# Attention and a mixture of experts in one hand-ordered kernel: weights loaded as eight halves, a later queue wait, another order

## The chip, the cores and the metric

The kernel runs on one core of one Trainium2 chip. The core has five engines with instruction queues of their own: TensorE (PE in the profile; its weight loads are PEld), VectorE (DVE), ScalarE (ACT), GpSimd (POOL) and SyncE (SP). Transfers are issued by an engine and carried out by 16 DMA engines. The metric is device time in microseconds (us), lower is better, as the median of several runs.

## What is computed

Eight sequences of 576 positions with 8 heads of 64 go through attention within a window of 32 positions to either side. The result, as 4608 rows of 512, goes through a mixture of experts: each row takes the expert with the largest router logit, to which a bias of the row's modality (0 or 1) is added.

```python
# q, k, v: [8, 8, 576, 64]
mask = np.abs(pos[:, None] - pos[None, :]) <= 32
attn = softmax(np.where(mask, q @ k.T / 8, -1e9))
x = (attn @ v).transpose(0, 2, 1, 3).reshape(4608, 512)
# modality_id: [4608], w_gate: [512, 8], modality_bias: [2, 8]
logits = x @ w_gate + modality_bias[modality_id]
e_idx, gate_w = argmax(logits, 1), max(softmax(logits))
# w1: [8, 512, 1024], w2: [8, 1024, 512]
for e in range(8):
    m = e_idx == e
    out[m] = gate_w[m, None] * (np.maximum(x[m] @ w1[e], 0) @ w2[e])
```

## The kernel before

With these inputs the bias decides the expert: all rows of one modality go to one expert. So two of the eight experts are loaded (`sp_i` holds which), and rows are sorted by modality. A flag computed on the chip would start a general path if this were not so; it isn't taken here.

**Tokens.** All work stands in a table, `ORDER`, of some 840 tokens. A loop at L891 to L893 reads them one by one and calls the function of that name with its numbers; a letter behind a slash is the engine (a, v, p), and digits behind a colon are banks of PSUM. Each engine runs its instructions in the order of this table; nothing reorders them. Waits between engines follow from which instruction reads what another has written. For this, the program is built on address ranges of the tiles.

The tokens, with b the sequence (batch), g one of its two head groups, t a tile of 256 rows (even t: expert 0, odd t: expert 1; t = 18 is a tile of rest):

- `l b.u.g` (L211) loads a half of q (u = 0) or k (u = 1), 288 KB, `lv b.i` (L216) a half of v, `W which.i` (L754) the weights: `W1.0`, `W1.1`, `W2.0`, `W2.1` are w1 and w2 of the two experts, 1 MB each as bf16 in `w1_sb` and `w2_sb`; `W1.2` and `W2.2` are those of the tile of rest. `Kg` (L248) loads the router's weights. All are issued by GpSimd, in the table's order. They take eight DMA lanes in turn (DMASW0 to 7 where an order is shown), and a transfer waits until the one before on its lane has landed.
- `t` (L540, DVE) transposes a load of q or k. `MA b.g`, `MB b.g` (L546 to L553, TensorE) write a band mask into banks ahead of scores, `SA`, `SB` (L572, TensorE) are the scores of a group, `sa`, `sb` (L580, L584, ACT) their exponentials into `pt`. A group without MA and MB has its exponentials multiplied with a mask on DVE instead: `M it` (L599), where it is two heads. `V it` (L618, TensorE) is attention times v, `v it` (L628, L629, DVE) the normalisation.
- `o b` (L531) builds one-hot matrices, `H b.m` (L638, TensorE) sorts rows of x with them, and `a b.m` (L656, ACT) copies the result to `xl`. `J` (L670) and `j` (L678) do the same for row numbers, to `cl`.
- `G k` (L708, L711, TensorE) are router logits, `r k.i` (L729 to L745) and `E k` (L751) the gate.
- `U t.mp` (L783) is a quarter of a tile's up-projection, eight matmuls of 128x256 over four slices of 128 (kd) of the 512; quarters 0 and 1 read the first 512 of the 1024 columns of w1, quarters 2 and 3 the others. `u` is its relu on ACT (L798) or DVE (L796).
- `D t.s.half` (L806) is half of the down-projection of 128 rows, four matmuls of 128x512; half 0 reads the first four of eight slices of w2. `y` scales by the gate on ACT (L834) or DVE (L836), `O` (L842, GpSimd) scatters 128 rows to the output from one of six buffers (`NYS`).
- `X i` (L887) are two filler matmuls on zeros. `N` is a drain of GpSimd: it waits there until what that engine has queued is done. `K..` are constants.

In the table `W1.0` stands behind `lv1.0`, `W1.1` behind `l2.0.1`, `W2.0` behind `lv2.1`; `U0.0` is the first up-projection, `U1.2` the first of expert 1, and `D0.0.0` the first down-projection. `N` stands ahead of `W2.2` and `W1.2`, towards the end.

## Time and profile before

| what | value |
| --- | --- |
| runs | 216.41 us median of 3 (216.21 to 216.47) |
| profiled execution | 214.1 us |
| its span, first to last instruction | 212.5 us |
| granted clock, mean | 0.988 |
| last matmul starts | 203.79 us, four of 128x512 in 1.04 us |
| last scatter | issued at 205.87 us, for 0.98 us |

The profile comes from one execution; its own time is 214.1 us, and the span is what its instructions cover. The 2.3 us to the median is the distance of that execution from the runs. Times in the rows below count from the span's start.

The page's slices (40 equal ones, busy tenths) show where the engines are full: TensorE from the fifth slice to the last but two, DMA through the first half.

```profile
PE   2877779899999999999999999999999999999950
DVE  6799999898988799878899883696547344303610
ACT  4588798898498989676897968665631221422220
POOL 7989989962934459999970442043021152743650
DMA  4999999999999999899996141022010995212431
```

### The profile page before, as it was taken

What the parts mean: (1) busy time and instruction counts of PE and PEld (TensorE: products, weight loads), DVE (VectorE), ACT (ScalarE), POOL (GpSimd) and SP (SyncE); (2) the same over time, 40 slices, a digit from 0 to 9 for tenths busy, and PEclk for the clock granted to TensorE, in tenths of its full rate; (3) what the DMA queues carried; (4) which work ended last, traced back from release to release, by engine and by line L of the source; (5) the groups of instructions that cost most, each with busy time, mean ns of one, the idle gap of its engine ahead of it and who ended that gap; (6) DMA issues with size and microseconds to landing.
All of it is one profiled execution on the core that took longest, in us unless ns stands there. A gap on an engine that the chain in (4) does not pass through costs nothing.

```text
span 212.5 us, 6219 instructions
## 1 busy us (share of the span) xinstructions
PE 192.7 (91%) x2525; PEld 137.0 (64%) x2552; DVE 152.1 (72%) x300; ACT 134.8 (63%) x229; POOL 119.2 (56%) x207
## 2 busy tenths in 40 slices
PE   2877779899999999999999999999999999999950
PEld 0444558688656887757885786578776676765620
DVE  6799999898988799878899883696547344303610
ACT  4588798898498989676897968665631221422220
POOL 7989989962934459999970442043021152743650
PEclk9999999999999999999999999999999999999995
DMA  4999999999999999899996141022010995212431
GB/s 70 189 187 185 205 175 214 185 190 212 212 188 185 181 226 297 164 149 206 86 210 141 50 150 49 3 99 103 3 49 3 158 221 214 102 49 96 153 106 61
DMA packets 47109, 30.43 MB, mean 143 GB/s; under 512 B 38712, under 2 KB 38752, under 8 KB 46688
## 3 DMA queue, kind: packets, MB, share of 16 engines
q0 software_dynamic: 46848, 29.90, 86.9%
q8 instruction: 22, 0.36, 0.7%
q14 instruction: 15, 0.12, 0.2%
q1 hardware_dynamic: 224, 0.05, 0.1%
HBM read 40.96 MB, written 9.70 MB: 238 GB/s over the span
## 4 chain that ended last, share of the span: by engine, by line
PE 65%; DMA 16%; POOL 9%; issue 4%; DVE 3%; POOLq 0%; DVEq 0%
PE banks L806 25%; PE banks L783 25%; DMA vt<-in_v_dram 9%; PE banks L618 5%; POOL oh L531 5%; PE banks L572 4%; DMA qkin<-in_q_dram 4%; DMA qkin<-in_k_dram 3%; PE banks L638 3%; DVE qk L540 2%; PE banks L708 2%; POOL qkin L211 1%; POOL out_dram L842 1%; POOL vt L216 1%; PE banks L670 1%
## 5 line engine op out<-in xcount | busy, mean ns | idle before, releaser
L783 PE MATMUL banks<-xl,w_sb 128*128 128x256 bf16 x576 | 70.8, 273 | 1.1 <-ACT xl L656 1.0
L806 PE MATMUL banks<-w_sb,hT 128*128 128x512 bf16 x266 | 67.3, 379 | 1.2 <-issue 0.2
L842 POOL DMA_INDIRECT out_dram<-ys,ix x37 | 38.4, 1039 | 52.7 <-issue 26.7
L783 PEld LDWEIGHTS <-w_sb 128*128 128x128 bf16 x576 | 54.3, 98 | 12.7 <-issue 1.6
L580 ACT ACTIVATE pt<-banks 128x1536 bf16<-128x1536 f32 x32 | 46.3, 1451 | 13.5 <-PE banks L572 13.4
L806 PEld LDWEIGHTS <-hT 128*128 128x128 bf16 x296 | 26.9, 98 | 24.9 <-issue 0.5
L540 DVE STREAM_TRANSPOSE qk<-qkin 128x576 int32<-128x576 int32 x32 | 39.3, 1248 | 2.4 <-DMA qkin<-in_k_dram 1.6
L599 DVE TENSOR_TENSOR pt<-pt,mask 128x1920 bf16<-128x1920 bf16 x30 | 34.0, 1150 | 3.0 <-ACT pt L580 3.0
L798 ACT ACTIVATE hT<-banks 128x512 bf16<-128x512 f32 x38 | 21.8, 598 | 19.3 <-PE banks L783 19.1
L796 DVE TENSOR_SCALAR hT<-banks 128x512 bf16<-128x512 f32 x36 | 24.3, 686 | 13.0 <-PE banks L783 11.8
L656 ACT CAST xl<-banks 128x704 f32 (+1 forms) x40 | 28.3, 707 | 4.6 <-DVE lo L729 2.2
L834 ACT ACTIVATE ys<-banks,gw 128x512 f32<-128x512 f32 x24 | 16.3, 688 | 19.3 <-PE banks L806 13.4
L629 DVE TENSOR_TENSOR xt<-banks,recs 128x640 bf16<-128x640 f32 x32 | 26.4, 825 | 1.2
L618 PEld LDWEIGHTS <-pt 128*128 128x128 bf16 x576 | 21.0, 97 | 4.7 <-issue 1.5
L618 PE MATMUL banks<-vt,pt 128*128 128x65 bf16 x576 | 22.6, 193 | 1.3 <-ACT pt L580 0.5
L216 POOL DMA_DIRECT2D vt<-in_v_dram x16 | 20.2, 1267 | 2.6 <-PE banks L572 1.1
L572 PE MATMUL banks<-qk 32*128 32x192 bf16 (+1 forms) x640 | 19.2, 240 | 2.5 <-DVE lpf L452 0.8
L531 POOL TENSOR_SCALAR oh<-io_l,lpf 128x128 bf16<-128x128 bf16 x30 | 20.2, 696 | 0.1
L572 PEld LDWEIGHTS <-qk 32*128 32x128 bf16 x640 | 12.6, 93 | 9.8 <-issue 5.3
L836 DVE TENSOR_SCALAR ys<-banks,gw 128x512 f32<-128x512 f32 x13 | 9.7, 744 | 12.8 <-PE banks L806 11.0
L678 ACT CAST cl<-banks 4x176 f32 (+1 forms) x40 | 11.4, 284 | 7.4 <-PE banks L670 6.8
L638 PE MATMUL banks<-oh,xt 128*128 128x128 bf16 (+1 forms) x160 | 13.0, 215 | 0.7 <-DVE xt L629 0.6
(157 smaller groups left out, 156.6 us busy)
## 6 DMA issues: line engine op xcount, KB each, us to landing
qkin<-in_q_dram POOLq DMA_DIRECT2D x16, 288.0 KB, 7.9
qkin<-in_k_dram POOLq DMA_DIRECT2D x16, 288.0 KB, 8.4
vt<-in_v_dram POOLq DMA_DIRECT2D x16, 288.0 KB, 7.7
w_sb<-in_moe_w_dram POOLq DMA_DIRECT2D x4, 1024.0 KB, 13.8
pt<-in_moe_w_dram POOLq DMA_DIRECT2D x2, 1024.0 KB, 10.1
out_dram<-ys,ix POOLq DMA_INDIRECT x37, 3.6
mid<-in_moe_modality_id_dram SPq DMA_DIRECT2D x3, 8.0 KB
mid<-in_moe_modality_id_dram SPq DMA_DIRECT2D x2, 6.0 KB
```

The source lines that it names most:

```text
L531: gp.tensor_scalar(out=t_[:, m, :], in0=io_l[:], scalar1=lpf[:, NM * b + m:NM * b + m + 1], scalar2=None, op0=ALU.is_equal)
L540: nc.vector.transpose(qk_t[b % 2][:, g, at:at + S].rearrange("p (t r) -> p r t", r=R), Ct["l", b, u, g][:].bitcast(I32).rearrange("p (r j) ...
L572: nc.tensor.matmul(st[:, h, WIN * i_:WIN * i_ + w_], qk[32 * h:32 * h + 32, c_, QK + k0:QK + k0 + P], qk[32 * h:32 * h + 32, c_, q0:q0 + w ...
L580: nc.scalar.activation(pt[:, :, 2 * part:2 * part + 2, 0:WIN], st[:, :, 0:2 * WIN].rearrange("p h (j c) -> p h j c", c=WIN), ACT.Exp, scal ...
L599: by[eng or "v"].tensor_tensor(out=p_ap, in0=p_ap, in1=mask[:], op=ALU.mult)
L618: nc.tensor.matmul(o_ap, pt[:, c1:c1 + P], vt[:, g0 + j, 0:D + 1], start=(m == 0 and i_ == 0), stop=(i_ == len(mine) - 1), skip_group_chec ...
L629: nc.vector.tensor_tensor(out=x_t[b % NX][:, :, P * hp:P * hp + P].rearrange("p m (h d) -> p h m d", h=2), in0=o_v[:, :, :, 0:D], in1=rec. ...
L656: ins = nc.scalar.copy(windows(xl, n_kd, P, NM * b + m), src)
L783: ins = nc.tensor.matmul(ph[:, u_, :], w1[:, kd, 2 * P * (mi // 2) + mi % 2:2 * P * (mi // 2 + 1):2], xl[:, kd, c0:c0 + n_], start=(kd == ...
L796: nc.vector.tensor_scalar(out=o_ap, in0=i_ap, scalar1=0.0, scalar2=None, op0=ALU.max)
L806: nc.tensor.matmul(Ct["D", t_, s_], Ct["h", t_][:, kf, P * s_:P * s_ + P], w2[:, kf, :], start=(kf == 0), stop=(kf == n_kf - 1))
L842: ins = nc.gpsimd.indirect_dma_start(out=out, out_offset=bass.IndirectOffsetOnAxis(ap=ix[:, k_, n_:n_ + 1], axis=0), in_=Ct["y", t_, s_][: ...
```

## The change

**Weights in halves.** `W_` takes one more number, h. For w1, h is the columns 512 h to 512 h + 511 of all four kd slices; a partition of `w1_sb` holds four rows of 1024 columns, so half h is four pieces of 512 in it, and the pieces of the two halves alternate. For w2, h is four of the eight slices, which stand together. Without h (`W1.2`, `W2.2`) the load is whole, as before.

```diff
-    def W_(_, which, i):
+    def W_(_, which, i, h=None):
         if ("er", i) not in T:
             T["er", i] = reg(sp_i[0:1, i:i + 1], [ET.Pool], 0, E - 1)
-        e_reg = T["er", i]
+        f_ = slice(0, F) if h is None else slice(F // 2 * h, F // 2 * (h + 1))
+        e_ = bass.ds(T["er", i], 1)
         if which == 1:
-            load_w(w1x if i == 2 else w1_sb[:, i], moe_w1, e_reg, W1P)
+            dst = w1x if i == 2 else w1_sb[:, i]
+            nc.gpsimd.dma_start(dst[:, :, f_], moe_w1[e_, :, f_].rearrange("a (ki ko) f -> ki (a ko) f", ki=P))
         else:
-            load_w((w2x if i == 2 else w2_sb[:, i]).rearrange("p (c e) d -> p c (e d)", e=2), moe_w2, e_reg, W2P)
+            dst = w2x if i == 2 else w2_sb[:, i]
+            dst = dst[:, f_.start // P:f_.stop // P].rearrange("p (c e) d -> p c (e d)", e=2)
+            nc.gpsimd.dma_start(dst, moe_w2[e_, f_, :].rearrange("a (c ki e) d -> ki (a c) (e d)", ki=P, e=2))
```

**The order.** The whole table is new: 846 tokens for 842. Two lines of it, around the first weights:

```diff
-V1:45 Kc3 lv1.0 W1.0 o0/p o1/p lv1.1 v1 V0:67 v0 SA0.1:0123 sa0.1 X7:4 SB1.0:4567 X8:3 X4:0 sb1.0 SA1.0:0123 t1.1.0 M2
+Kc4 Kr2 V1:67 Ky0 Kq1/a lv0.1 l2.1.0 v1 sa0.1 l2.0.0 lv1.0 Kc2 o0/p W1.0.1 Kc3 lv1.1 W1.1.0 V0:45 Ko0 SB1.0:0123 X11:6
...
-N Kf3:5 D11.0.0:1 D10.0.0:2 U13.3:3 u13.3/v r6.5 U12.2:4 G7:6 r7.0 G8:0 D10.0.1:2 D11.0.1:1 r8.5 Kf4 U12.3:3 D13.1.0:5
+y12.0/v r7.5 O12.0 O12.1 r7.6 W2.2 N G9:4 r7.1 r7.2 Z0 u13.3/v D13.0.0:5 U14.0:7 U17.0:3 U14.2:6 D13.1.0:2 E7 r7.3 r7.4
```

Beside the weights: group 1 of sequence 0 gets its mask on TensorE (`MA0.1`, `MB0.1` are new, `M2`, `M3` are gone); `N` stands behind `W1.2` and `W2.2`; the two one-hot matrices that DVE built (`o4`, `o7`) go to GpSimd, one pad (`Kp2`) from ACT to DVE; the relus are 37 and 37 on ACT and DVE instead of 38 and 36, with several of `u` and `y` on the other engine; the fillers are 14 tokens as before, 7 of them ahead of the first scores instead of 3. Behind the edit, lines of the changed kernel are 1 higher from the table on, and the weight loads are L765 (w1) and L769 (w2).

GpSimd, from the first weights on, in the kernel before (the buffers with their numbers: w1_sb_86 is the tile of both w1, qkin4 the fifth load buffer, vt2 the v of sequence 2, wg_sb the router's weights):

```order
L754 DMA w1_sb_86<-in_moe_w1_dram 128x4096 [waits DMASW0_49]
L211 DMA qkin3_72<-in_k_dram 128x1152 [waits DMASW1_49]
L211 DMA qkin4_73<-in_k_dram 128x1152 [waits DMASW2_49]
L216 DMA vt2_83<-in_v_dram 128x18x64 [waits DMASW3_49]
L248 DMA wg_sb_105<-in_moe_w_gate_dram 128x32 [waits DMASW4_49]
L531 TENSOR_SCALAR oh2_101<-io_l_118,lpf_127 128x128 x5
L211 DMA qkin5_74<-in_q_dram 128x1152 [waits DMASW5_49,DVE_49]
L216 DMA vt2_83<-in_v_dram 128x18x64 [waits DMASW6_49]
L754 ISA
L754 DMA w2_sb_87<-in_moe_w2_dram 128x4x1024 [waits DMASW7_49]
```

The same place in the changed kernel, from `W1.1.0` on (the second half of w1 here is `W1.0.0`, the third `W1.1.1`; `W1.0.1` stands eight rows ahead, on lane 5):

```order
L765 DMA w1_sb_86<-in_moe_w1_dram 128x4x512 [waits DMASW7_49]
L212 DMA qkin2_71<-in_q_dram 128x1152 [waits DMASW0_49]
L765 ISA
L765 DMA w1_sb_86<-in_moe_w1_dram 128x4x512 [waits DMASW1_49]
L217 DMA vt2_83<-in_v_dram 128x18x64 [waits DMASW2_49]
L212 DMA qkin3_72<-in_k_dram 128x1152 [waits DMASW3_49]
L532 TENSOR_SCALAR oh1_100<-io_l_118,lpf_127 128x128 x5
L249 DMA wg_sb_105<-in_moe_w_gate_dram 128x32 [waits DMASW4_49]
L212 DMA qkin4_73<-in_q_dram 128x1152 [waits DMASW5_49]
L212 DMA qkin5_74<-in_k_dram 128x1152 [waits DMASW6_49]
L765 ISA
L765 DMA w1_sb_86<-in_moe_w1_dram 128x4x512 [waits DMASW7_49]
```

Two halves stand where the second w1 stood, and `W1.1.1` has moved behind one v half, the router's weights and two loads of sequence 3; `W2.0.1`, `W2.0.0` and then `lv2.1` follow it.

TensorE at the first up-projection of the kernel before (`U0.0`, behind the scores `SB2.0`), and then at the first of expert 1 (`U1.2`):

```order
L572 MATMUL banks<-qk_77 128x128
L783 LDWEIGHTS w_sb [waits DMASW5_49]
L783 MATMUL banks<-xl,w_sb 128x256 [waits Activation_49]
L783 LDWEIGHTS w_sb
...
L783 LDWEIGHTS w_sb [waits DMASW0_49]
L783 MATMUL banks<-xl,w_sb 128x256 [waits Activation_49]
L783 LDWEIGHTS w_sb
```

The same two places in the changed kernel, `U0.3` and `U1.0`:

```order
L784 LDWEIGHTS w_sb [waits DMASW5_49,DMASW1_49]
L784 MATMUL banks<-xl,w_sb 128x256 [waits Activation_49]
L784 LDWEIGHTS w_sb
...
L784 LDWEIGHTS w_sb [waits DMASW7_49]
L784 MATMUL banks<-xl,w_sb 128x256 [waits Activation_49]
L784 LDWEIGHTS w_sb [waits DMASW7_49]
L784 MATMUL banks<-xl,w_sb 128x256
```

Where one lane stood at the first up-projection, now two stand (5 and 1); where one lane stood once at the first of expert 1, lane 7 now stands in the first and again in the second weight load, each time for one more transfer on it.

TensorE at the first down-projection, `D0.0.0`, of the changed kernel, behind the scores `SA3.0` (`hT` holds the relu's result):

```order
L573 MATMUL banks<-qk_78 128x192
L807 LDWEIGHTS hT_90
L807 MATMUL banks<-w_sb,hT_90 128x512 [waits DMASW1_49]
L807 LDWEIGHTS hT_90
L807 MATMUL banks<-w_sb,hT_90 128x512
```

Lane 1 is that of `W2.0.0` at this place; `W2.0.1` is on lane 0, for which `D0.1.1` waits further down.

More of the change, by code (lines that the diff above doesn't have):

```diff
@@ new lines @@
+l2.0.1 W1.0.0 lv2.0 l2.1.1 v0 t1.1.0 t1.1.1 sb1.0 SA1.0:4567 V2:01 v2 V3:23 sa1.0 SB1.1:4567 v3 sb1.1 t2.0.0 M5 t2.0.1
+M4 SA1.1:0123 H0.3:4 H0.0:6 H0.4:7 sa1.1 a0.0 H0.1:5 X12:0 H0.2:1 a0.1 a0.2 a0.3 a0.4 V5:23 X2:0 V4:56 v5 SB2.0:0123
+o1/p Kg l3.0.0 l3.1.0 W1.1.1 U0.3:7 U0.2:4 v4 Kr3/v M6 M7 sb2.0 W2.0.1 Kc5 Ky1 W2.0.0 lv2.1 V6:56 u0.2/a u0.3/a
+SA2.0:0123 sa2.0 v6 U1.0:4 V7:56 J0:01 U1.1:2 lv3.0 l4.1.0 u1.0/a t2.1.0 j0.0 j0.1 j0.2 j0.3 u1.1/a v7 Kp2/v l3.0.1
+l3.1.1 o2/p W2.1.0 M9 M8 Kc8 H1.4:7 H1.0:5 U0.0:4 J1:23 H1.1:6 j0.4 a1.0 j1.0 a1.1 j1.1 u0.0/v V9:01 H1.2:5 a1.2 j1.2
@@ L85 @@
+O15.0 u17.3/v O14.1 u18.0/v D17.1.0:5 U16.2:3 D18.0.0:0 D17.1.1:5 D18.0.1:0 D16.1.0:1 r8.3 r8.4 y17.1/v Z3 u16.2/v
+y18.0/a r8.6 O17.1 r9.6 O18.0 D17.0.0:4 D16.1.1:1 D17.0.1:4 D16.0.0:0 y17.0/v Z4:2 Z5 D16.0.1:0 y16.1/a y16.0/a O16.1
+O17.0 O16.0
 """
```

84 lines of the change are left out of this document (37 added, 47 removed).

## The prediction

> **What bounds the kernel now.** I read the page's busy rows first, then the windows by stage, then the waits of TensorE, then the timeline around the places where it waits.
>
> ```profile
> span 212.5 us, 6219 instructions
> PE 192.7 (91%) x2525; PEld 137.0 (64%) x2552; DVE 152.1 (72%) x300; ACT 134.8 (63%) x229; POOL 119.2 (56%) x207
> 9.17:52.64 43.47, 37.65 (x700) 28.99 (x704) 40.59 (x69) 37.71 (x56) 35.93 (x72) 1.00 1.44 194
> 52.64:66.00 13.36, 13.04 (x150) 7.49 (x149) 11.69 (x19) 10.20 (x20) 8.80 (x20) 1.00 1.48 195
> 66.00:110.00 44.00, 43.58 (x681) 33.56 (x683) 37.92 (x62) 36.31 (x62) 34.70 (x51) 1.00 1.44 188
> 110.00:150.00 40.00, 39.63 (x568) 28.91 (x567) 30.76 (x50) 28.60 (x52) 11.64 (x16) 1.00 0.29 89
> 150.00:204.83 54.83, 54.38 (x439) 36.23 (x443) 23.96 (x79) 16.58 (x31) 19.26 (x27) 1.00 0.39 107
> PE banks L618 <- DMA vt<-in_v_dram: 0.2, 1, 0.2
> PE banks L806 <- issue: 0.2, 1, 0.2
> ```
>
> A window row gives its stretch, its length, then the busy time and count of PE, PEld, DVE, ACT and POOL, the granted clock, the DMA share and GB/s. From 52.64 us on TensorE is busy 160.6 of 162.2 us up to 204.83, in every stage about 99%, and the last two rows (its waits from 52.7 us to the end) are all it waits there: 0.2 and 0.2 us. So from the first down-projection at 52.64 us on, the end is set by how much TensorE work is left. An edit counts if it changes that work, or the moment at which TensorE gets there. Ahead of it there are 5.8 us of idle TensorE time since 9.17 us, and DMA runs at 194 GB/s through all of that stage.
>
> ```profile
> 31.50 1.69 PE L783 MATMUL banks<-xl,w_sb 128*128 128x256 bf16 x14 [0.31 <-ACT xl L656]
> 39.10 1.92 PE L783 MATMUL banks<-xl,w_sb 128*128 128x256 bf16 x16 [0.70 <-ACT xl L656]
> 52.64 0.38 PE L806 MATMUL banks<-w_sb,hT 128*128 128x512 bf16 x1
> 30.55 0.61 POOL L754 DMA_DIRECT2D w_sb<-in_moe_w_dram  x1 [0.75 <-issue]
> w_sb<-in_moe_w_dram POOLq DMA_DIRECT2D x1, 1024.0 KB, 8.5
> 38.74 0.78 POOL L754 DMA_DIRECT2D w_sb<-in_moe_w_dram  x1
> w_sb<-in_moe_w_dram POOLq DMA_DIRECT2D x1, 1024.0 KB, 13.8
> ```
>
> These are the three moments that matter: the first up-projection at 31.50, the first one of the second expert (U1.2) at 39.10, and the first down-projection (D0.0.0) at 52.64. The weights set them. The second w1, issued at 30.55, lands 8.5 us later, at 39.05; TensorE starts on it at 39.10. The first w2, issued at 38.74, lands at 52.5, just ahead of 52.64.
>
> **The change, part by part. First the halves.** A half helps if each up-projection waits for its own half alone. The order of instructions in the part on the change says otherwise for w1. A half of w1 is one half of each of four rows of a partition, so the two halves interleave in address, and the first weight load of U0.3 names two DMA lanes: that of W1.0.1, which it reads, and that of W1.0.0, which it doesn't read. U1.0 names lane 7 twice, in two neighbouring weight loads: W1.1.0 used that lane, and W1.1.1 used it next. So U1.0, which reads W1.1.0 alone, also waits for W1.1.1. For w2 the halves are contiguous, and D0.0.0 names one lane. When do these halves land? The queue is saturated, so I count what stands ahead in it.
>
> ```profile
> 27.86 0.56 POOL L211 DMA_DIRECT2D qkin<-in_q_dram  x1
> qkin<-in_q_dram POOLq DMA_DIRECT2D x1, 288.0 KB, 6.3
> 36.92 8.78 DMA qkin<-in_q_dram
> 31.16 1.08 POOL L211 DMA_DIRECT2D qkin<-in_k_dram  x2
> qkin<-in_k_dram POOLq DMA_DIRECT2D x2, 288.0 KB, 10.2
> 32.22 1.25 POOL L216 DMA_DIRECT2D vt<-in_v_dram  x1
> vt<-in_v_dram POOLq DMA_DIRECT2D x1, 288.0 KB, 11.6
> 33.44 0.57 POOL L248 DMA_DIRECT2D wg_sb<-in_moe_w_gate_dram  x1
> wg_sb<-in_moe_w_gate_dram POOLq DMA_DIRECT2D x1, 8.0 KB, 10.5
> ```
>
> W1.0.0 has the same transfers ahead of it as the q half l2.0.1 of before, with one half of the other expert's w1 (W1.1.0) besides. l2.0.1 landed at 27.86 + 6.3 = 34.2; the whole second w1 took from there to 39.05, 4.9 us, so half of it is 2.45, and **W1.0.0 lands at about 36.6**. W1.1.1 is the last of exactly the set of transfers that ended before with l3.0.0, and that (a row of the chain of waits) landed at 36.92 + 8.78 = 45.70. So **W1.1.1 lands at about 45.7**, if halves cost half. Does a transfer carry a fixed price in this queue? Kg, of 8 KB, landed at 33.44 + 10.5 = 43.9, and the v half ahead of it at 32.22 + 11.6 = 43.8: at most 0.12 us, so two more transfers ahead of W1.1.1 cost at most 0.24, and I take nothing. The Trainium skill ("DMA: Bandwidth & Descriptors", section "Anatomy of one DMA — SWDGE (gpsimd) path") gives every such DMA a fixed 2.0 us beside its bytes; paid in full by the two more it would put W1.1.1 at 49.7 and the time 4 us higher. The Kg row doesn't show it behind a full queue, so I leave it out.
>
> **The two stalls.** U0.3 would be ready at about 31.5, where the first up-projection stands now, and waits to 36.6. Behind it up to U1.0 stand two up-projections, one attention product and one score group, about 2.8 us, so TensorE comes to U1.0 at 39.4 and stands still until 45.8: about 6.4 us. All others queue behind it on TensorE, and DVE and ACT run dry. The first stall is swallowed by the second: U1.0 ends it at 45.8 wherever the first left it. From there to D0.0.0 the work is as follows, against the stretch from U1.2 to D0.0.0 of before.
>
> ```profile
> 39.10:52.64 13.54, 13.50 (x252) 11.53 (x252) 12.54 (x24) 11.83 (x21) 7.77 (x16) 1.00 1.50 196
> L783 PE MATMUL banks<-xl,w_sb 128*128 128x256 bf16 x72 | 8.9, 273 | 0.7 <-ACT xl L656 0.7
> 71.14 1.85 PE banks L783 x16
> 82.94 0.25 PE banks L670 x5
> 78.95 0.22 PE banks L638 x4
> 46.52 0.24 PE L708 MATMUL banks<-wg_sb,xl 128*128 128x8 bf16 x4
> 47.02 0.71 PE L618 MATMUL banks<-vt,pt 128*128 128x65 bf16 x18
> ```
>
> Before, 13.54 us held 9 up-projections (72 matmuls of 128x256), 3 attention products, 4 score groups, 2 router groups and 1 J. After, it is 12 up-projections, 3 attention products, 4 score groups, 1 router group, 2 J and 5 H. Three up-projections more at 1.85 / 2 = 0.9 (the pieces that stand closer are 0.87) are +2.7; a J +0.25; five H at about 0.2 +1.0; a router group less is -0.5 (46.52 to 47.02). That is 13.54 + 3.45 = 17.0, of which the first matmul (0.1) is done. ACT has to hand over five H and ten J copies in the same stretch; I put 0.3 on that. D0.0.0 then stands at 45.8 + 16.9 + 0.3 = 63.0, if TensorE runs at its usual pace after standing still.
>
> Does it? The trace shows one start from rest.
>
> ```profile
> 4.18 1.04 PE L887 MATMUL banks<-zero_b 128*128 128x512 bf16 x2 [4.18 <-DVE one_f L258]
> 6.72 1.91 PE L887 MATMUL banks<-zero_b 128*128 128x512 bf16 x4
> 10.55 1.04 PE L887 MATMUL banks<-zero_b 128*128 128x512 bf16 x4
> PEclk9999999999999999999999999999999999999995
> ```
>
> Four equal filler matmuls take 1.91 us at 6.72 and 1.04 at 10.55: spaced 0.43 against 0.22, half the pace, though the granted clock's digits are 9 from the first slice. The slow rows last from 4.18 to 8.6, 4.4 us, and so cost about 2.2; up to where the next fast rows stand it could be 2.7. After 6 us of rest in mid-kernel the cost lies between 0 (nothing in the trace shows a second slow start, since no rest after 9.2 us is longer than 0.8 us) and 2.7; I take 1.5. The Trainium skill ("TensorE: Matmul & The Clock Gate", section "What's actually happening") says why: the array falls to half its clock after an idle window of about 3.4 us and comes back after as much work. By that page the second stall, of over 6 us, would do it, at an estimated 1.7 us; by the rows alone it is open. So **D0.0.0 at 64.5, 11.8 us later than 52.64.**
>
> **Behind D0.0.0.** Ahead of it stood 13 up-projections, 11 attention products and 2 router groups; now 14, 10 and 1. Behind it remain 0.55 + 0.5 - 0.9 = about +0.2 us, and the 0.2 that TensorE waited for a v half goes, since that has long landed. The sum stays.
>
> **What costs nothing.**
>
> ```profile
> 11.42 0.81 PE L549 MATMUL banks<-neg,ident 128*128 128x384 bf16 x4
> 6.29 0.63 PE L553 MATMUL banks<-neg,ident 128*128 128x128 bf16 x4
> L599 DVE TENSOR_TENSOR pt<-pt,mask 128x1920 bf16<-128x1920 bf16 x30 | 34.0, 1150 | 3.0 <-ACT pt L580 3.0
> ```
>
> The two groups masked on TensorE instead of by DVE add four wide mask matmuls twice and four narrow ones, at most 2 x 0.81 + 0.63 = 2.25 us of TensorE, and take two multiplies of 1.15 us from DVE. Both lie ahead of the first up-projection, where TensorE idles and then stalls, so neither reaches the end. Without that cover the masks would cost up to their 2.25 us. The fillers keep their number; their new places are ahead of the stalls too. One-hot work that goes from DVE to GpSimd, a pad from ACT to DVE, and the relu and scale steps that change engine lie beside a full TensorE, which now waits 0.4 us in 150: a step of 0.6 to 0.7 us more on an engine that is 86% busy at the most (DVE, 37.92 of 44.00) fits. Uncovered, each would cost that much once. N, the wait of GpSimd for its own queue, now stands behind the loading of W2.2 instead of ahead of it: queued behind it are index casts and scatters. No row shows what N takes. Between a gain of 0.5 us (W2.2 starts sooner, but the last token tile isn't waited for at 204) and a loss of 2 (scatters late, their six buffers full, the down-projections held), I take 0, as the waits after 52.7 us are nearest.
>
> **The sum.** 214.1 (the profiled execution) + 11.8 = 225.9. The median of the runs is 216.41, 2.3 above that execution, so 228.2.
>
> **The rivals.**
> (a) The forecast, a stall to 45.8 and then a slow start: 228.2. Chance 0.48.
> (b) The stall, but TensorE at full pace behind it, and the hand-offs hidden: D0.0.0 at 62.6 to 63.0, time 226.4 to 226.8. For it: no slow row after 10 us anywhere in the trace. Chance 0.25.
> (c) Halves of w1 are dearer than half: their runs are half as long. The far bound is the rate of a v half, which comes in the smallest pieces here: lv2.0 landed 1.9 us after the k half ahead of it (the second k half, issued at 31.7, landed 10.2 us later, at 41.9). That makes 3.4 us of 512 KB against 2.45; four such halves put W1.1.1 up to 3.8 late, and the time at 229 to 232. Chance 0.13.
> (d) The other side: **the halves do release their readers separately**, as the change says. Then U0.3 starts at 31.5 as now, U1.0 at about 34.3, and D0.0.0 after 16.9 more at 51.2; W2.0.0 lands at about 51, since one v half of 1.9 us now stands behind it instead of ahead. That is 1.4 earlier, less 0.2 of work behind: 215.2. It decides from D0.0.0 ahead of 52.64 on, that is if U1.0 starts before some 35.7. Against it stand the second lane of U0.3 and the doubled lane 7 of U1.0. Chance 0.05, of which 0.04 faster and 0.01 within 0.2%.
> (e) The stall as forecast, and the new order brings waits of its own later (N, scatters, relus that changed engine): 2 to 4 us more, 230 to 232. Against it: DVE and ACT come out of the stall with nothing queued. Chance 0.09.
>
> **How the numbers follow.** The likeliest is (a), 228.2. The range takes in (b) at its lower end with 1 us for the landing time of W1.1.1, and (c) and most of (e): 225.4 to 231.5. A measurement of this kernel can tell about 0.2% (0.4 us) from no change. Faster 0.04, same 0.01, slower 0.95.
>
> **What would show it.** In the profile after: the weight load of the first up-projection waits for the w_sb DMA to about 36.6, that of U1.0 (its second one) to about 45.8, one long idle of TensorE of some 6 us; matmuls of 128x256 spaced 0.22 instead of 0.11 us just behind it, for (a), or not, for (b); the first 128x512 down-projection at about 64.5; nearly no wait of TensorE after that. If the first down-projection stands before 52.6, step one, on the lanes, is wrong. If W1.1.1 lands after 47, the price of a half is.

## The result, and the profile after

The changed kernel takes 231.86 us (median of 6 runs, 229.65 to 233.09) against 215.72 (median of 6, 214.28 to 216.47) of the kernel before: **ratio 1.0725, 95% interval 1.0649 to 1.0802**. That is slower, as forecast. The forecast was 228.2 with a range of 225.4 to 231.5; 1.0725 times 215.72 is 231.4, at the very end of it, and the bare median lies 0.4 above. So the sign and the main mechanism came out, and some 3 us were missing.

The page of the profile after, with the rows that answer to those shown of before:

```profile
span 231.2 us, 6243 instructions
PE 197.7 (86%) x2537; PEld 139.6 (60%) x2564; DVE 149.9 (65%) x298; ACT 135.4 (59%) x227; POOL 133.0 (58%) x221
PE   7875644399999998969999999999999999999910
PEclk9999995759999999999999999999999999999995
DMA  5999999999990059999939938000313079522441
```

Three things stand there at once. TensorE has a hole in the slices 6 to 8 (29 to 46 us). The granted clock, 9 in every slice of before but the last, falls to 5 and 7 in the slices 7 to 9. And DMA, which never rested before 110 us, rests in the slices 13 and 14 (69 to 81 us).

The profiled execution took 233.09 us, with a span of 231.2; before it was 214.1, with a span of 212.5. The first is the longest of its kernel's six runs and the second lies below all six of the other's, so 18.7 us lie between the two traces and 16.1 between the medians. I split the 18.7 us by two marks that both traces have, the first down-projection (`D0.0.0`) and the last matmul. `e3_n_early` below, traced at 229.78 us, has the first two stretches within 0.8 us of these, so they don't rest on one execution. The timeline of TensorE after (start, length, the work, idle before it and what ended that):

```profile
38.10 3.43 PE L784 MATMUL banks<-xl,w_sb 128*128 128x256 bf16 x16 [6.55 <-DMA w_sb<-in_moe_w_dram]
42.47 0.28 PE L784 MATMUL banks<-xl,w_sb 128*128 128x256 bf16 x1
46.78 1.68 PE L784 MATMUL banks<-xl,w_sb 128*128 128x256 bf16 x7 [4.02 <-DMA w_sb<-in_moe_w_dram]
65.72 1.90 PE L807 MATMUL banks<-w_sb,hT 128*128 128x512 bf16 x7
219.71 1.04 PE L807 MATMUL banks<-w_sb,hT 128*128 128x512 bf16 x4
```

| stretch | before | after | more |
| --- | --- | --- | --- |
| start to `D0.0.0` | 52.64 | 65.72 | +13.08 |
| `D0.0.0` to the end of the last matmul | 152.19 | 155.03 | +2.84 |
| last matmul to the end of the span | 7.67 | 10.45 | +2.78 |

The first stretch is the two stalls: 6.55 us at `U0.3`, then one single matmul of `U1.0` at 42.47, and 4.02 us at its second one. This is the doubled lane of the order rows, seen in time: the second weight load of `U1.0` waited for `W1.1.1`, which `U1.0` doesn't read.

What follows the stalls is seen in the windows (stretch, length, busy time and count of PE, PEld, DVE, ACT and POOL, granted clock, DMA share, GB/s):

```profile
38.00:41.40 3.40, 3.30 (x18) 2.37 (x19) 0.00 (x0) 0.00 (x0) 2.31 (x5) 0.52 1.20 204
46.78:50.00 3.22, 3.22 (x32) 2.72 (x33) 0.48 (x2) 0.72 (x2) 3.22 (x7) 0.50 1.42 193
52.00:65.72 13.72, 13.72 (x234) 11.56 (x232) 12.18 (x20) 11.57 (x22) 5.47 (x9) 1.00 1.38 201
```

Behind each stall TensorE runs at half its clock, for 3.4 us at 38.0 and for some 4.5 us from 46.78 (0.63 still in 50 to 52), and then at 1.00. TensorE is "busy" all the while, so the page's busy share hides this; the clock's column shows it. The Trainium skill ("TensorE: Matmul & The Clock Gate", section "What's actually happening") gives half the clock after an idle window of about 3.4 us; with 0.50 and 0.52 behind rests of 4.0 and 6.5 us the trace agrees. Other runs below show the fall behind rests of 2 us and of less than 1 us as well, so here it doesn't take a single rest of 3.4 us.

The two other stretches are GpSimd's. Its timeline after:

```profile
76.75 1.17 POOL L744 CAST ix<-ixf 128x4 int32<-128x4 f32 x1 [17.63 <-DVE ixf L741]
191.18 0.84 POOL L769 DMA_DIRECT2D pt<-in_moe_w_dram  x1
203.99 1.03 POOL L843 DMA_INDIRECT out_dram<-ys,ix  x1 [11.97 <-ACT hT L799]
224.06 0.97 POOL L843 DMA_INDIRECT out_dram<-ys,ix  x1 [0.30 <-issue]
```

At 59 us GpSimd comes to the index cast of the second router group (`r1.6`) and stands 17.6 us, since that group's logits (`G1`) now stand on TensorE behind the first down-projections. Loads of q, k and v are queued behind the cast on GpSimd; that is the hole in the DMA digits. At 191 us it issues `W2.2`, comes to `N`, and does nothing for 12 us. The row puts the end of that down to a result of ACT; in the table `N` stands between the two rows, and `e3_n_early` below tells the two apart. What is late behind it then holds up the scaling, which waits for a buffer that a scatter frees, and so the next scatter:

```profile
208.15 0.75 DVE L837 TENSOR_SCALAR ys<-banks,gw 128x512 f32<-128x512 f32 x1 [2.64 <-DMA out_dram<-ys,ix]
```

The last scatter then starts 3.3 us behind the end of the last matmul (220.75), where it was 1.0 before. What TensorE waited for in the second stretch:

```profile
PE banks L619 <- DMA vt<-in_v_dram: 1.9, 1, 1.9
PE banks L709 <- ACT ys L835: 0.7, 1, 0.7
```

1.9 us for v, and 0.7 for a bank of PSUM that the router's logits are to go to and that ACT's scaling (`ys`) read late. That scaling had itself waited for a scatter to free its buffer, as ACT's timeline shows:

```profile
89.57 0.69 ACT L835 ACTIVATE ys<-banks,gw 128x512 f32<-128x512 f32 x1 [1.45 <-DMA out_dram<-ys,ix]
```

### The profile page after: what moved, and what is told of

Same layout as the page of the kernel before. It is cut to its first block, busy times and chain, and to the rows that moved or that the text cites. A ratio compares the mean times of both kernels' runs of the same rounds, so it can differ in the third digit from the quotient of the medians.

```text
span 231.2 us, 6243 instructions
## 1 busy us (share of the span) xinstructions
PE 197.7 (86%) x2537; PEld 139.6 (60%) x2564; DVE 149.9 (65%) x298; ACT 135.4 (59%) x227; POOL 133.0 (58%) x221
## 2 busy tenths in 40 slices
DMA packets 48965, 30.43 MB, mean 132 GB/s; under 512 B 38776, under 2 KB 40864, under 8 KB 48800
## 4 chain that ended last, share of the span: by engine, by line
PE 65%; DMA 13%; POOL 12%; issue 5%; DVE 1%; POOLq 0%; ACT 0%; DVEq 0%
PE banks L784 26%; PE banks L807 23%; PE banks L619 5%; DMA w_sb<-in_moe_w_dram 5%; PE banks L573 4%; POOL oh L532 4%; DMA vt<-in_v_dram 3%; POOL out_dram L843 3%; PE banks L639 3%; DMA qkin<-in_q_dram 3%; POOL qkin L212 2%; DMA out_dram<-ys,ix 2%; PE banks L709 1%; PE banks L671 1%; PE banks L888 1%
## 5 line engine op out<-in xcount | busy, mean ns | idle before, releaser
L784 PE MATMUL banks<-xl,w_sb 128*128 128x256 bf16 x576 | 74.8, 280 | 10.6 <-DMA w_sb<-in_moe_w_dram 10.6
L784 PEld LDWEIGHTS <-w_sb 128*128 128x128 bf16 x576 | 55.7, 100 | 23.8 <-DMA w_sb<-in_moe_w_dram 10.9
L807 PE MATMUL banks<-w_sb,hT 128*128 128x512 bf16 x264 | 68.2, 379 | 1.3 <-issue 0.2
L843 POOL DMA_INDIRECT out_dram<-ys,ix x37 | 41.8, 1129 | 37.7 <-issue 16.8
L541 DVE STREAM_TRANSPOSE qk<-qkin 128x576 int32<-128x576 int32 x32 | 39.4, 1250 | 2.4 <-DMA qkin<-in_q_dram 1.1
L797 DVE TENSOR_SCALAR hT<-banks 128x512 bf16<-128x512 f32 x37 | 25.1, 685 | 20.2 <-PE banks L784 19.9
L600 DVE TENSOR_TENSOR pt<-pt,mask 128x1920 bf16<-128x1920 bf16 x28 | 32.0, 1153 | 6.5 <-ACT pt L585 4.5
L532 POOL TENSOR_SCALAR oh<-io_l,lpf 128x128 bf16<-128x128 bf16 x40 | 27.3, 694 | 0.2
L744 POOL CAST ix<-ixf 128x4 int32<-128x4 f32 (+1 forms) x10 | 3.8, 382 | 35.0 <-DVE ixf L741 35.0
L629 DVE RECIPROCAL recs<-banks 128x10 f32<-128x10 f32 x32 | 6.8, 214 | 21.9 <-PE banks L619 21.2
```

Source lines behind the costliest of these rows:

```text
L532: gp.tensor_scalar(out=t_[:, m, :], in0=io_l[:], scalar1=lpf[:, NM * b + m:NM * b + m + 1], scalar2=None, op0=ALU.is_equal)
L541: nc.vector.transpose(qk_t[b % 2][:, g, at:at + S].rearrange("p (t r) -> p r t", r=R), Ct["l", b, u, g][:].bitcast(I32).rearrange("p (r j) ...
L600: by[eng or "v"].tensor_tensor(out=p_ap, in0=p_ap, in1=mask[:], op=ALU.mult)
L784: ins = nc.tensor.matmul(ph[:, u_, :], w1[:, kd, 2 * P * (mi // 2) + mi % 2:2 * P * (mi // 2 + 1):2], xl[:, kd, c0:c0 + n_], start=(kd == ...
L797: nc.vector.tensor_scalar(out=o_ap, in0=i_ap, scalar1=0.0, scalar2=None, op0=ALU.max)
L807: nc.tensor.matmul(Ct["D", t_, s_], Ct["h", t_][:, kf, P * s_:P * s_ + P], w2[:, kf, :], start=(kf == 0), stop=(kf == n_kf - 1))
```

## The experiments

The runs stood on several chips, and the kernel before has its own median on each (214.8, 220.3 and 216.0 us in the three groups below, beside 215.7 above). So kernels of one group are compared in us, and across groups by their ratio to the kernel before. The ratio doesn't seem to take the chip out altogether. From `D0.0.0` to the end of the last matmul the order of before takes 151.8 to 152.7 us in three traces outside group 2 and 156.4 in group 2 (`e8_before_halves`), 4 more; the new order with contiguous halves takes 155.6 in group 1 (`e1_apart`) and 156.9 in group 2 (`e5_apart_n`), 1 more.

### Group 1: the false wait, the order, N, the clock (kernel before: 214.84)

**`e1_apart`**: w1's halves as contiguous pieces, so that a half is a range of its own.

```diff
-    w1_sb = const.tile([P, 2, n_kd, F], BF16)
+    w1_sb = const.tile([P, 2, 2, n_kd, F // 2], BF16)
...
-            dst = w1x if i == 2 else w1_sb[:, i]
-            nc.gpsimd.dma_start(dst[:, :, f_], moe_w1[e_, :, f_].rearrange("a (ki ko) f -> ki (a ko) f", ki=P))
+            dst = w1x if i == 2 else w1_sb[:, i, h]
+            nc.gpsimd.dma_start(dst, moe_w1[e_, :, f_].rearrange("a (ki ko) f -> ki (a ko) f", ki=P))
...
+            w1, f0 = w1_sb[:, t_ % 2, mp // 2], F // 2 * (mp // 2)
```

> The changed kernel, with the same table; only the place of w1 in its tile is changed, so that a half is one contiguous piece and each up-projection waits for its own half alone. Theory (the stall is the wait for the half that isn't read, and the rest follows from it): the first up-projection starts at about 31.7 us instead of 38.1, U1.0 goes through at about 34.5 instead of 46.8, no stretch of half clock behind it, the first down-projection at about 52 instead of 65.7; GpSimd's wait for the index cast of the second router group (17.6 us) shrinks below 4 us, and the waits of TensorE for v and router banks behind it (1.9 and 0.7 us) go. Time about 215.6 if all of that comes back but the 2.8 us at the tail. Rival A (the order itself holds GpSimd at that cast, whatever TensorE does): the first down-projection at 52, but time about 218. Rival B (halves are late because they are dear, not because of the lanes): no change, about 231.9.

219.18 us, ratio 1.0142 (1.0057 to 1.0227). Each first weight load now names one lane. TensorE:

```profile
31.01 1.91 PE L787 MATMUL banks<-xl,w_sb 128*128 128x256 bf16 x16 [0.34 <-ACT xl L657]
34.01 1.05 PE L787 MATMUL banks<-xl,w_sb 128*128 128x256 bf16 x8
51.52 1.90 PE L810 MATMUL banks<-w_sb,hT 128*128 128x512 bf16 x7
```

The places are those expected within 0.7 us: 31.0, 34.0, 51.5 (expected 31.7, 34.5, 52), and the clock is 1.00 from 38 to 52 us. **The false wait makes 5.8 of the 7.25%, some 12.6 us.** The edit changes the layout of the tile as well, but both pages count the same 48965 packets of DMA, and `W1.1.1` takes 12.4 us from issue to landing in both kernels, so the load itself is no cheaper. The time is not all as the theory had it: 219.2 lies above 215.6 and above rival A's 218. The cast of `r1.6` waits 4.15 us in place of 17.6 (expected: below 4), but the waits of TensorE behind 52 us, which were expected to go, are still there, 1.5 us for v and 1.1 for a router bank. From `D0.0.0` to the end of the last matmul this trace has 155.6 us, 3.4 more than before; from there to the end it has 7.88, 0.2 more than before, although `N` stands late. So a part of the loss is in the order itself, even without the stall. Another part may be the clock: the traced execution took 216.71 us at a mean clock of 0.988, the other three 218.91 to 219.97 at 0.975 to 0.980. The last paragraph on the experiments has more on this.

**`e2_wholes`**: the new table with whole weights.

```diff
-W1.0.1 ... W1.1.0 ... W1.0.0 ... W1.1.1 W2.0.1 ... W2.0.0 ... W2.1.0 ... W2.1.1
+W1.0   ... W1.1   ...                   W2.0   ...            W2.1
```

> The changed kernel with its new table, but whole weights: each whole stands where the first half of that weight stood. Theory: no false wait; w1 of expert 1 as a whole lands at about 38 us and lets U1.0 through there instead of at 46.8; the first down-projection at 38 + 16.9 = 55, time about 218.5. Rival (the new order itself, not the halves, is what stalls): the first down-projection stays beyond 60 us and the time above 226.

222.74 us, ratio 1.0351 (1.0289 to 1.0412); expected 218.5. TensorE goes through `U1.0` at 37.51 and reaches the first down-projection at 55.98, 18.5 us behind it instead of 16.9:

```profile
37.51 1.89 PE L784 MATMUL banks<-xl,w_sb 128*128 128x256 bf16 x8 [1.94 <-DMA w_sb<-in_moe_w_dram]
```

The window of the first 1.8 us behind that wait:

```profile
37.50:39.30 1.80, 1.79 (x10) 1.30 (x11) 0.41 (x1) 0.00 (x0) 1.07 (x1) 0.50 2.12 164
```

The clock stands at 0.50 there, behind a wait of only 1.94 us. The rival, that the new order itself stalls beyond 60 us, falls. Against the trace of before this one has 3.3 us more up to the first down-projection, 4.4 from there to the end of the last matmul, and 1.7 behind it. In the middle stretch TensorE waits 2.0 us for v, at 91 us, and the clock falls to 0.50 once more behind that wait (0.50 in 92 to 94 us, 0.65 in 94 to 96). With whole weights the new order is still 3.5% slower than before: it brings expert 1 forward, and its w1 isn't there yet.

**`e3_n_early`**: `N` ahead of `W1.2` again.

```diff
-... Kf4 W1.2 ... W2.2 N G9:4 ...
+... Kf4 N W1.2 ... W2.2 G9:4 ...
```

> The changed kernel with N, GpSimd's wait for its queue, moved ahead of W1.2 as before. Theory (N behind W2.2 holds GpSimd until W2.2 has landed, and the scatters then queue up to the end): GpSimd's idle of 12 us at 192 to 204 us goes, the last scatter starts about 1 us behind the last matmul instead of 3.3, time about 2.8 us lower than the changed kernel, 229.1. Rival (the 12 us are the wait for a result of ACT, as the row names it, or the scatters are late for another reason): no change, 231.9 within 0.5.

229.01 us, expected 229.1; ratio 1.0638 (1.0576 to 1.0700). The interval overlaps that of the changed kernel, so the time alone doesn't settle it; the trace does. GpSimd, and then the last matmuls of TensorE:

```profile
191.09 0.84 POOL L769 DMA_DIRECT2D pt<-in_moe_w_dram  x1
192.23 1.03 POOL L843 DMA_INDIRECT out_dram<-ys,ix  x1 [0.30 <-issue]
221.57 0.97 POOL L843 DMA_INDIRECT out_dram<-ys,ix  x1 [0.36 <-ACT ys L835]
```

```profile
219.49 1.04 PE L807 MATMUL banks<-w_sb,hT 128*128 128x512 bf16 x4
```

The scatter that stood behind `N` goes out at once, and the last one 1.04 us behind the last matmul's end. From there to the end of the span (228.2) it is some 7.7 us, as in the kernel before: **between these two traces, the 2.8 us of the tail are `N`.** GpSimd's 12 us of idle don't go, though, as the theory had it. They stand further down, at 195 to 207 us, where the next result isn't scaled yet:

```profile
207.13 1.05 POOL L843 DMA_INDIRECT out_dram<-ys,ix  x1 [11.97 <-issue]
```

From there the scatters follow one another to the end, and they start at 207.13 us here and at 209.68 in the changed kernel. So what `N` costs is how much later that last row of scatters begins, not the 12 us, and it isn't the same everywhere: the other five traces of the new order with `N` late have tails of 7.9 to 10.3 us.

**`e4_warm`**: eight tokens of filler (16 matmuls) ahead of `U1.0`.

```diff
-... v6 U1.0:4 ...
+... v6 X14:7 X15:7 X16:7 X17:7 X18:7 X19:7 X20:7 X21:7 U1.0:4 ...
```

> The changed kernel with 16 more filler matmuls of 128x512 right ahead of U1.0 (about 3.5 us of work, inside the stall of 42.6 to 46.8 us). Theory (the half clock of 46.8 to 51.4 us comes from standing still): clock 1.00 behind the stall, the first down-projection about 2.3 us earlier, at 63.4, time 229.6. Rival (the half clock has another cause, or the clock falls whatever runs): 65.7 and 231.9, unchanged.

228.04 us, ratio 1.0604 (1.0527 to 1.0681), from the timeline and the windows:

```profile
41.63 3.61 PE L889 MATMUL banks<-zero_b 128*128 128x512 bf16 x15
45.53 0.94 PE L785 MATMUL banks<-xl,w_sb 128*128 128x256 bf16 x7 [0.18 <-DMA w_sb<-in_moe_w_dram]
62.61 1.90 PE L808 MATMUL banks<-w_sb,hT 128*128 128x512 bf16 x7
```

```profile
45.50:49.00 3.50, 3.42 (x51) 2.96 (x51) 1.91 (x4) 2.23 (x7) 3.50 (x8) 1.00 1.15 208
```

The same stall, filled with useless work, leaves the clock at 1.00, and the way from the end of the stall to the first down-projection takes 62.61 - 45.53 = 17.08 us instead of 65.72 - 46.78 = 18.94. **The half clock behind the second stall costs 1.9 us between these two traces**, and 1.2 to 2.4 if the same stretch of `e3_n_early` (18.32) and `e9_cast` (19.47) is taken for it. (The other 1.2 us by which the down-projection stands earlier are an earlier landing of the half in this execution.)

### Group 2: what adds up, and the parts alone (kernel before: 220.33)

**`e5_apart_n`** is the edits of `e1_apart` and `e3_n_early` together; **`e6_apart_n_cast`** has besides:

```diff
-... r1.6 o4/p l4.1.1 O0.1 ... O2.0 O0.0 l5.1.0 l5.0.0 lv4.0 ...
+... o4/p l4.1.1 ... l5.1.0 l5.0.0 lv4.0 r1.6 O0.1 O2.0 O0.0 ...
```

> The first experiment (w1 with contiguous halves) with N moved ahead of W1.2 besides. Theory (the false wait and N are two separate prices that add up): 2.8 us less than the contiguous halves alone, 219.2 - 2.8 = 216.4; the last scatter about 1 us behind the last matmul. Rival (what is left of that kernel's loss is all in the order of GpSimd's casts and loads, and N costs only behind the stall): 219, unchanged.

> As the one before (contiguous halves, N early), and on GpSimd the index cast of the second router group and the first three scatters stand behind four loads (two of k, one of q, one of v) that stood behind them. Theory (GpSimd waits 4 us at that cast with loads queued behind it, and TensorE pays for it later with 1.5 us for v and 1.1 us for a router bank): those waits go, 1 to 2.6 us less than the kernel without this move, about 214.2, and near the kernel before. Rival (the loads wait for DVE or for their lanes anyway, or the later scatters fill the six buffers): no change against the kernel without this move.

221.14 us, ratio 1.0022 (0.9987 to 1.0057), and 220.73 us, ratio 1.0012 (0.9971 to 1.0053). The absolute times of the expectations don't hold on this chip; by ratio, 216.4 / 214.84 = 1.007 was expected of the first and 0.997 of the second. On this chip, then, **the changed kernel without the false wait and with `N` early is level with the one before.** That `N` made the step from 1.0142 to 1.0022 isn't shown: the two ratios come from different chips, their intervals touch (1.0057), and the traces have it the other way round, with a tail of 7.9 us in `e1_apart` and 9.2 in `e5_apart_n`. The last scatter starts 3.0 us behind the last matmul here, not 1, since ACT's last scaling starts 2.0 us behind it. The move of the cast shows no difference beyond the intervals. It does what it should, and it doesn't pay. The waits of TensorE from the first down-projection on, first without it, then with it:

```profile
PE banks L619 <- DMA vt<-in_v_dram: 1.4, 2, 1.0
PE banks L709 <- ACT ys L838: 1.1, 1, 1.1
```

```profile
PE banks L573 <- ACT pt L585: 2.7, 4, 1.2
PE banks L573 <- DVE xt L630: 0.4, 1, 0.4
```

The waits for v and the router's bank are gone, and waits of the scores for ACT's exponentials and DVE stand in their place: 2.5 us went, 3.1 came; a wait of 1.0 to 1.1 us for DVE stands in both and is left out here. The order of before waits for those exponentials as well on this chip, 0.9 us in `e7_before_n_late` and 1.1 in `e8_before_halves`.

**`e7_before_n_late`**: the kernel before with `N` behind `W1.2`.

```diff
-... O11.1 N Kf3:5 ... W2.2 ... W1.2 r6.6 ...
+... O11.1 Kf3:5 ... W2.2 ... W1.2 N r6.6 ...
```

> The kernel before with only N moved, behind W2.2 and W1.2. Theory (N holds GpSimd until W1.2 has landed, about 165 + 10 = 175 us, and delays the four scatters that stood at 172 to 176 by some 3 us; 30 us before the end that is made good): the same time within 0.5 us, 214.8. Rival (N's place costs its 2.8 us wherever it stands behind these loads): 217.6.

222.15 us, ratio 1.0078 (1.0044 to 1.0113): +1.7 us, between the two theories, and neither. GpSimd, then TensorE:

```profile
169.28 1.39 POOL L755 DMA_DIRECT2D pt<-in_moe_w_dram  x2 [6.29 <-PE banks L784]
182.73 0.18 POOL L744 CAST ix<-ixf 128x4 int32<-128x4 f32 x1 [12.06 <-DVE sm L737]
```

```profile
190.04 1.03 PE L784 MATMUL banks<-xl,w_sb 128*128 128x256 bf16 x8 [1.63 <-ACT hT L799]
```

Again GpSimd stands 12 us behind weight loads, here 30 us ahead of the end, and by the tail it is made good: from the last matmul to the end of the span it is 7.7 us. TensorE waits 1.6 us for a relu of ACT at 190, and 0.3 more close by, while five late scatters go out; in `e8_before_halves`, with the same order there but `N` early, it is busy for 11.89 of the 12 us from 183 to 195, here for 10.01. So the 1.7 us stand at that place. But no scaling step of ACT or DVE waits for a scatter in this run, so what ties that wait to `N` isn't shown; what is shown is that the late place isn't free here either, and that it doesn't cost the 2.8.

**`e8_before_halves`**: the kernel before, each whole as two halves in succession.

```diff
-... lv1.0 W1.0 o0/p ...
+... lv1.0 W1.0.0 W1.0.1 o0/p ...
```

> The kernel before, its table unchanged but for each whole weight replaced by its two halves, one behind the other, in the form of the change (interleaved for w1). Theory (a half costs half, and a false wait costs nothing where both halves stand together): the same time within 0.5 us, 214.8. Rival (each DMA of this kind has a fixed price of some 2 us in the queue): the four more DMAs ahead of the first down-projection move it by up to 6 us, time 217 to 221.

223.54 us, ratio 1.0156 (1.0100 to 1.0213). **The theory fell**: this kernel is slower, though nothing in it waits for a wrong half. The windows of 28 to 33 us, first of `e7_before_n_late` on the same chip, then of this kernel, and its weight wait:

```profile
28.00:33.00 5.00, 4.22 (x75) 3.40 (x73) 4.88 (x10) 4.94 (x6) 4.14 (x12) 1.00 1.56 172
```

```profile
28.00:33.00 5.00, 4.21 (x80) 3.42 (x80) 4.88 (x9) 4.94 (x6) 4.89 (x10) 1.00 1.04 108
```

```profile
42.80 1.91 PE L784 MATMUL banks<-xl,w_sb 128*128 128x256 bf16 x16 [1.95 <-DMA w_sb<-in_moe_w_dram]
```

The DMA queue ran dry: 108 GB/s for 172. So the rival's reason, a price of each DMA in a full queue, isn't what is seen. GpSimd issued the loads too late: its ten one-hot steps took 9.17 us (7.58 in `e7_before_n_late`), and each weight has two issues. The first down-projection came at 56.31 instead of 53.00. `e12_before_w2_halves` below has halves for w2 alone, the same slow one-hot steps and the same gap in the DMA (50 GB/s at 29 to 31 us), and its first down-projection stands at 54.38. So between these traces some 1.9 us at most are left for the halves of w1.

### Group 3: the cast, the place of the half, the masks, w2 alone (kernel before: 215.98)

**`e9_cast`**: the changed kernel with only the move of `e6_apart_n_cast`.

```diff
-... r1.6 o4/p l4.1.1 O0.1 ... O2.0 O0.0 l5.1.0 l5.0.0 lv4.0 ...
+... o4/p l4.1.1 ... l5.1.0 l5.0.0 lv4.0 r1.6 O0.1 O2.0 O0.0 ...
```

> The changed kernel with one move on GpSimd: the index cast of the second router group and the first three scatters stand behind the four loads (two k, one q, one v) that stood behind them. Theory (GpSimd stands 17.6 us at that cast, the DMA queue runs dry, and TensorE later waits 1.9 us for v and 0.7 us for a router bank): from the first down-projection to the last matmul about 2.5 us less (now 155.0 us from 65.7 to 220.75), time about 1.1% lower, ratio to the kernel before about 1.061. Rival (the loads wait anyway, or the later scatters cost what is gained): ratio unchanged at 1.0725.

225.53 us (225.41 to 229.01), ratio 1.0438 (1.0332 to 1.0543), more than expected. Its profiled execution took 228.46, 1.058 of 215.98, as expected. GpSimd, then TensorE:

```profile
62.47 1.27 POOL L218 DMA_DIRECT2D vt<-in_v_dram  x1
75.83 1.17 POOL L745 CAST ix<-ixf 128x4 int32<-128x4 f32 x1 [12.09 <-DVE ixf L742]
```

```profile
64.80 1.90 PE L808 MATMUL banks<-w_sb,hT 128*128 128x512 bf16 x7
215.95 1.04 PE L808 MATMUL banks<-w_sb,hT 128*128 128x512 bf16 x4
```

GpSimd still stands at the cast, 12 us, but the loads went out ahead of it. From the first down-projection to the end of the last matmul it is 216.99 - 64.80 = 152.19 us, where the changed kernel has 155.03 and the kernel before 152.19. **So the +2.84 of the second stretch are the loads behind the cast.** It holds for the other traces too: the six of the new order with the cast early, outside group 2, have 154.6 to 156.6 us there. Three of the five runs took 225.4 to 225.5 us, 3 less than the profiled one; why stays open.

**`e10_w111`**: `W1.1.1` right behind `W1.0.0`.

```diff
-l2.0.1 W1.0.0 lv2.0 l2.1.1 ... Kg l3.0.0 l3.1.0 W1.1.1 U0.3:7 ...
+l2.0.1 W1.0.0 W1.1.1 lv2.0 l2.1.1 ... Kg l3.0.0 l3.1.0 U0.3:7 ...
```

> The changed kernel with W1.1.1 issued right behind W1.0.0, ahead of one v half, two loads of q and k, the router weights and two more loads. The false wait stays. Theory (the stall lasts until the half that isn't read has landed, so it moves with its place in the queue): W1.1.1 lands 2.6 us behind W1.0.0, at about 40.7 instead of 46.8; U1.0 goes on there, the first down-projection at about 58.5 to 59.5, ratio about 1.04. Rival (the loads put behind it now hold TensorE as long): the first down-projection beyond 63, ratio above 1.06.

224.78 us, ratio 1.0396 (1.0311 to 1.0482), as expected. `U1.0` goes through at 41.18 with no wait, and the first down-projection stands at 58.43. The false wait is still in the program; it costs what the place of the unread half in the queue makes of it. The wait at `U0.3` is still there as well.

**`e11_before_masks`**: the kernel before with `MB0.1`, `MA0.1` in place of `M2`, `M3`.

```diff
-... Kb/a SB0.1:0123 ... SA0.1:0123 ... t1.1.0 M2 M3 l2.0.1 ...
+... Kb/a MB0.1:0123 SB0.1:0123 ... MA0.1:0123 SA0.1:0123 ... t1.1.0 l2.0.1 ...
```

> The kernel before with the masks of group 1 of sequence 0 on TensorE instead of DVE, nothing else. Theory (both lie where TensorE and DVE have room ahead of the first up-projection): no change within 0.4 us, ratio 0.998 to 1.002. Rival (the masks stand in the way of the first scores): 1.5 to 2.3 us more, ratio 1.007 to 1.011.

214.21 us (213.87 to 214.82), **ratio 0.9926 (0.9889 to 0.9963): 0.7% less than the kernel before**, by an interval that leaves 1 out, and better than the theory. The runs of before on that chip spread from 214.58 to 217.63 us, those of this kernel from 213.87 to 214.82. TensorE:

```profile
52.94 1.02 PE L807 MATMUL banks<-w_sb,hT 128*128 128x512 bf16 x3
203.65 1.04 PE L807 MATMUL banks<-w_sb,hT 128*128 128x512 bf16 x4
```

These places are those of the kernel before within 0.3 us (52.64, 203.79), as is `U1.2` (39.40 for 39.10), and the two profiled executions are alike too, 214.02 and 214.1 us. So what is gained isn't in any trace here, and its reason stays open.

**`e12_before_w2_halves`**: the kernel before with halves for w2 alone.

```diff
-... W2.0 ... W2.1 ...
+... W2.0.0 W2.0.1 ... W2.1.0 W2.1.1 ...
```

> The kernel before with the two w2 in halves, one behind the other; w1 stays whole. Theory (what cost 1.6% with all four in halves is w1, whose halves are written in four times as many pieces and delay GpSimd's next work): no change within 0.5 us, ratio below 1.003. Rival (each DMA more costs about 0.85 us, whatever its shape): two more DMAs ahead of the place where it counts, 1.7 us, ratio about 1.008.

215.38 us, ratio 0.9970 (0.9932 to 1.0008): no loss. So two DMAs more as such cost nothing here, and by the two medians it is w1's halves that cost in `e8_before_halves` (four runs, on another chip). But the reason that I gave, that their pieces delay GpSimd's next work, isn't shown: the ten one-hot steps took 9.22 us here too, behind a whole w1.

**The clock ahead of the first up-projection.** One more thing stands in the traces with the new order. The granted clock in 40 slices, first in `e1_apart`, then in `e5_apart_n` and `e10_w111`:

```profile
PEclk9999999999999999999999999999999999999995
PEclk9958969999999999999999999999999999999995
PEclk9999887999999999999999999999999999999995
```

In seven of the nine traces with the new order the granted clock falls to about 0.50 somewhere ahead of the first up-projection (0.54 from 28.0 to 31.7 us in `e5_apart_n`, 0.50 from 26.3 to 29.6 in `e10_w111`), though TensorE's longest rest in the microseconds before those falls is 0.81 us. It doesn't fall there in the changed kernel's trace and that of `e1_apart`, nor in any of the five traces with the order of before. Where a stall follows, the stall swallows it. Where none follows, the first up-projection comes later, at 33.61 us in `e5_apart_n` and 32.39 in `e6_apart_n_cast`, both in group 2, for 31.01 in `e1_apart` in group 1. So the new order seems to have a price of 1.4 to 2.6 us in some executions, for which the prediction has no term. What sets the fall off isn't shown: up to there `e1_apart` and `e4_warm` (0.52 from 27 to 29 us) run the same work on TensorE at nearly the same times.

## Why the prediction came out, and where it was off

**What bounds the kernel.** It held. From the first down-projection on TensorE is full, and each microsecond ahead of it reaches the end; `e1_apart`, `e2_wholes` and `e10_w111` moved that mark to 51.5, 56.0 and 58.4 us, and their ratios follow in that order (1.014, 1.035, 1.040). The prediction's own rows add to 150.6 busy of 152.2 us, not 160.6 of 162.2; the 99% stands.

**The two lanes.** The step that decided. Predicted: `U0.3` at 36.6 and the second matmul of `U1.0` at 45.8; measured 38.10 and 46.78. `e1_apart` takes the false wait away and gets 12.6 us back.

**The landing of the halves.** Right within 0.5 us in two traces, 1.0 to 1.5 short in two others with the same loads: the waits for 36.6 and 45.8 ended at 36.86 and 45.53 in `e4_warm`, 36.83 and 45.33 in `e9_cast`, but 38.10 and 46.78 in the changed kernel and 37.93 and 46.60 in `e3_n_early`. So this distance is a spread between executions, whose cause is open, and not a price of a half; rival (c) isn't needed for it.

**The work behind the stall.** 16.9 us predicted plus 0.3 for hand-offs; `e4_warm` at full clock took 17.08. `D0.0.0`, forecast at 64.5, stood at 65.72, and at 64.92 in `e3_n_early` and 64.80 in `e9_cast`.

**The slow start.** 1.5 us taken, between 0 and 2.7; `e4_warm` gives 1.9 (1.2 to 2.4 by the other traces). That the clock would fall is shown by its column, which I had thought wouldn't show it: at the start of the program it stands at 1.00 while the fillers run at half pace, in mid-kernel it says 0.50. One detail was off with it: TensorE came to `U1.0` at 42.5 instead of 39.4, since the first stall ended 1.5 us later and the work behind it was at half clock as well, and so the second rest was 4.0 us long, not 6.4. That cost nothing, as `U1.0` couldn't go before 46.8.

**Behind the first down-projection.** Here the prediction failed: "The sum stays", and between the two traces it grew by 2.84 + 2.78. The first part is steady, 2.4 to 4.4 us in the six traces of this order outside group 2, and the move of the cast takes it away. The second is not: with `N` late the tail is longer by 0.2 us (`e1_apart`) to 2.8. For `N` I had a range that ended at 2 us and by the right mechanism (scatters late, buffers full), and I took 0, because the waits of before behind 52.7 us were 0.2 us. Those rows show TensorE with `N` in its old place; they say nothing on GpSimd standing 12 us behind a load. Counting what stands behind `N` on GpSimd, at that load's own time to landing (10.1 us is the page's median for those two loads before), would have shown that wait. The cast of `r1.6` I didn't list at all: `G1` moved behind the down-projections on TensorE, the cast that needs it stayed ahead of four loads on GpSimd, and the stall stretched that wait to 17.6 us. It is rival (e), "the stall as forecast, and the new order brings waits of its own later", with 2 to 4 us and a chance of 0.09, which came true beside (a), with 5.6 us between the traces. That 231.4 still lies inside the range, by 0.1 us, is partly luck: the range took most of (e) in, but the sum had nothing for it.

**What costs nothing.** Right for the masks, and on the good side: alone they gain 0.7%, for a reason that no trace shows. The one-hot work, the pad and the relus that changed engine were not tried alone. Without the false wait and with `N` early the whole is level with before (1.0022), but on the chip of group 2 only, where the order of before is slowed; so that they cost little is argued, not shown.

## What to carry to other kernels

A load cut in halves releases the reader of one half only if each half is one range of addresses of its own: look in the instruction order at how many lanes the first reader waits for, before looking at the time. On an engine that issues transfers, each instruction that waits for a late result (a cast, a drain) holds every transfer queued behind it; count its wait against what stands behind it, not against how busy the engine is. A stall of the matmul engine costs more than its length, since work starts at half clock behind it; filling it with useless matmuls brought 1.9 us back. Before a term is called mis-sized, read the same place in several traces: the landing of the halves moved by 1.5 us between kernels with the same loads, and the price of `N` from 0.2 to 2.8.

## What the runs showed of the hardware

- The granted clock fell to 0.50 behind waits of 1.94 and 1.98 us (`e2_wholes`), and at 26 to 32 us in `e5_apart_n` and `e10_w111` with no rest above 0.81 us ahead of it. So the length of one rest doesn't decide it; what does isn't shown. It came back to 1.00 after 3.2 us of work in `e10_w111` (36.78 to 40.0) and after some 4.5 in the changed kernel. With 16 filler matmuls in the rest it stayed at 1.00 (`e4_warm`).
- A drain of GpSimd behind the issue of a 1 MB load held that engine for 12 us, until about 2 us behind the load's landing in the changed kernel (issued at 191.18, landed 10.7 us later, next scatter at 203.99).
- The five one-hot steps of one sequence take 2.95 us in most places and 3.2 to 4.9 in others; single steps of 0.59 us then last up to 2.4. Which step it hits changes from kernel to kernel, and with it the moment at which the loads behind it are issued.
- The kernel before has medians of 214.8, 220.3 and 216.0 us on the chips of the three groups. Differences of 1% mean nothing across them without the ratio, and the ratio may shift with the chip too, if it slows two orders unlike (4 us against 1 in the stretch given ahead of group 1).
